# Ones multiplied in the early waits of TensorE, and a new order of 4,646 steps, in an attention and gated-MLP kernel

## The chip, the cores and the metric

The kernel runs as one program on one core of a Trainium2 chip. The metric is the device time of one execution in microseconds (us). A change is judged by the median of several executions.

## The reference

For each of 8 batches: attention over 8 heads of 576 tokens with 64 numbers each, in which only scores within tau of a row's maximum are kept, and then a gated MLP on the joined heads (576 x 512).

```python
scores = scale * np.matmul(q, k.transpose(0, 1, 3, 2))
thresh = np.max(scores, axis=-1, keepdims=True) - tau
scores = np.where(scores >= thresh, scores, -1000000000.0)
attn = softmax(scores)                    # over the last axis
x = np.matmul(attn, v)                    # heads joined: 576 x 512
h = gelu_tanh(x @ w_in)                   # 576 x 1024
u, v = h[..., :512], h[..., 512:]
v_n = layer_norm(v) * g_ln
gated = u * (np.einsum('ts,bsd->btd', w_sg, v_n) + b_sg[None, :, None])
out = x + gated @ w_out
```

## The kernel before, in words

The work of attention is cut into 32 pairs of heads, four pairs to a batch. A pair n goes through these steps, named as in the plan: q and k are loaded (L520) and v (L525); POOL scales q (q_scale, L528) and copies the last 64 tokens of both heads into one tile (L533); TensorE makes the scores in five blocks (s, L552, and the tail block, L559); VectorE (DVE) takes each block's row maxima (nm, L568), POOL turns them into thresholds (thr, L572), ScalarE (ACT) selects (sel, L582, which reads PSUM and frees the bank) and takes exponentials (exp, L588); DVE transposes 32 x 32 blocks (dt, L636); DMAs on SP's queue carry the transposed blocks to DRAM and back into other partitions (put, L646, and get, L653, in two parts: swa and swb); TensorE multiplies by v in two steps (pv, L667). The inverse sums take a way of their own: a small transpose (idt, L601), a write to DRAM (L606) and four reads back (L611, L618). DVE scales with them (rmul, L675 and L677), ACT and POOL split the result into a high and a low part (xh, L682; xl, L685; xt, L688). These x tiles of four pairs feed the batch's MLP, which TensorE works off in pieces of four products (L759), or for the first units of batch 0 in two parts (L775), so that the part on the first three pairs can go ahead of the fourth pair.

The weights w_in and w_out arrive as 64-bit words and are turned into pairs of 32-bit parts by ACT, POOL and DVE (L398 to L439); for six of the w_in tiles TensorE adds the parts with three products against identity matrices (w_sum, L430). All of this is done once, during the first 150 us.

Nothing schedules itself: the plan is a list of 4,646 steps, and the table ORDER gives the order in which their instructions are issued to the engines' queues; the table PLACES gives each TensorE step its PSUM bank or banks. Within an engine the instructions run in this order; across engines semaphores make them wait. Sixteen steps of the plan ("warm", L994) multiply a tile of ones with itself; nobody reads their result. They lie in columns 0 to 255 of a bank, which are also columns of the score blocks (columns 0 to 287), so that such a product waits for the reader of the scores that were there.

Of the kernel before, what the change touches and what calls it, by code (L numbers as in the profile page):

```python
# [12 lines left out]
F32 = mybir.dt.float32  # L13
# [7 lines left out]
P = 128  # L21
# [221 lines left out]
def tile_threshold_attention_gated_mlp(  # L243
# [15 lines left out]
    nc = tc.nc  # L259
# [15 lines left out]
    RG = P // BLK  # L275
    HB = BLK // 2
    MAINQ = NM * BLK
    PBUFS = 10
    COLS = 4
    GROUPS = 4  # L280
    PAIRS = CHUNKS // 2
# [711 lines left out]
    def warm_up(i):  # L993
        return lambda: nc.tensor.matmul(bank(f"warm{i}")[:, 0:256], warm[:, 0:P], warm, start=True, stop=True)  # L994
# [60 lines left out]
```

## Time and profile before

| | |
|---|---|
| median of 3 executions | 856.62 us (856.04 to 858.21) |
| the profiled execution | 859.3 us, span 857.5 us |
| TensorE (PE) busy | 815.6 us, 95% of the span |
| DVE, ACT, POOL busy | 632.2, 638.5, 467.2 us |
| mean granted TensorE clock | 0.992 |

The profiled execution is 2.7 us slower than the median. TensorE's busy time in 40 slices of 21.4 us is 7 or 8 tenths in five of the first six slices and 9 tenths or more in nearly all later ones. "PEld" is TensorE's loading of weights. Each product of 32-bit numbers shows as two records in the profile.

### The profile page before, as it was taken

What the parts mean: (1) busy time and instruction counts of PE and PEld (TensorE: products, weight loads), DVE (VectorE), ACT (ScalarE), POOL (GpSimd) and SP (SyncE); (2) the same over time, 40 slices, a digit from 0 to 9 for tenths busy, and PEclk for the clock granted to TensorE, in tenths of its full rate; (3) what the DMA queues carried; (4) which work ended last, traced back from release to release, by engine and by line L of the source; (5) the groups of instructions that cost most, each with busy time, mean ns of one, the idle gap of its engine ahead of it and who ended that gap; (6) DMA issues with size and microseconds to landing.
All of it is one profiled execution on the core that took longest, in us unless ns stands there. A gap on an engine that the chain in (4) does not pass through costs nothing.

```text
span 857.5 us, 24743 instructions
## 1 busy us (share of the span) xinstructions
PE 815.6 (95%) x9726; PEld 663.8 (77%) x9726; DVE 632.2 (74%) x1130; ACT 638.5 (74%) x1346; POOL 467.2 (54%) x797
## 2 busy tenths in 40 slices
PE   7787898999999899999999999999999989999998
PEld 4454677887888778887788878887688878888898
DVE  5998699776869477885878658884887738786255
ACT  6977588876979488895988768886798649877271
POOL 3786389443753465534664447534573347634283
PEclk9998999999999999999999999999999999999999
DMA  8898763885776934886558844888366953588401
GB/s 281 239 270 218 204 171 91 223 220 130 184 196 188 233 103 119 228 232 176 140 152 199 236 118 133 223 231 221 113 161 174 244 161 91 152 226 219 103 15 63
DMA packets 218998, 151.74 MB, mean 177 GB/s; under 512 B 32257, under 2 KB 204289, under 8 KB 218882
## 3 DMA queue, kind: packets, MB, share of 16 engines
q1 hardware_dynamic: 218882, 150.16, 65.5%
q8 instruction: 76, 1.25, 0.6%
q14 instruction: 40, 0.33, 0.1%
HBM read 97.68 MB, written 52.43 MB: 175 GB/s over the span
## 4 chain that ended last, share of the span: by engine, by line
PE 58%; DMA 14%; DVE 8%; POOL 6%; SPq 5%; issue 4%; ACT 4%; DVEq 0%; POOLq 0%; ACTq 0%
PE all_banks L759 34%; PE all_banks L552 11%; PE all_banks L667 9%; DMA pt<-swb 5%; DMA ir<-ird 3%; PE all_banks L559 3%; DVE columns L568 3%; DVE pt L636 2%; SPq L653 2%; DMA swb<-pt 2%; SPq L646 2%; DMA ird<-ir 1%; ACT p L582 1%; ACT p L588 1%; DMA out_T<-ot 1%
## 5 line engine op out<-in xcount | busy, mean ns | idle before, releaser
L568 DVE TENSOR_REDUCE columns<-all_banks 128x1 f32<-128x576 f32 x288 | 206.3, 745 | 70.2 <-PE all_banks L552 50.8
L582 ACT ACTIVATE p<-all_banks,columns 128x576 f32<-128x576 f32 x288 | 201.8, 737 | 70.9 <-POOL columns L572 69.5
L636 DVE STREAM_TRANSPOSE pt<-p 128x576 f32<-128x576 f32 x288 | 208.2, 753 | 22.0 <-ACT p L588 15.2
L588 ACT ACTIVATE p<-p,columns 128x576 f32<-128x576 f32 x288 | 220.9, 771 | 0.6
L552 PE MATMUL all_banks<-rk,rq 64*64 64x288 f32 x2048 | 165.9, 417 | 10.4 <-ACT p L582 6.0
L667 PE MATMUL all_banks<-pt,rv 64*64 64x128 f32 (+1 forms) x4608 | 158.1, 284 | 11.6 <-DMA pt<-swb 9.8
L667 PEld LDWEIGHTS all_banks<-pt,rv 64*64 64x64 f32 x4608 | 145.0, 133 | 25.5 <-issue 13.1
L572 POOL TENSOR_TENSOR columns<-columns 128x2 f32<-128x2 f32 (+1 forms) x160 | 35.0, 219 | 205.7 <-DVE columns L568 204.3
L552 PEld LDWEIGHTS all_banks<-rk,rq 64*64 64x64 f32 x2048 | 77.4, 133 | 63.3 <-ACT p L582 20.2
L759 PE MATMUL all_banks<-wsh,z 128*128 128x288 f32 (+2 forms) x512 | 114.2, 303 | 2.1 <-DVE uu L738 1.5
L759 PE MATMUL all_banks<-x,wi 128*128 128x288 f32 (+2 forms) x720 | 115.1, 300 | 0.0
L759 PE MATMUL all_banks<-wi,x 128*128 128x512 f32 (+1 forms) x424 | 112.9, 402 | 0.9 <-POOL x L685 0.8
L759 PEld LDWEIGHTS all_banks<-x,wi 128*128 128x128 f32 x720 | 101.1, 188 | 13.5 <-issue 5.9
L759 PE MATMUL all_banks<-gh,wo 128*128 128x288 f32 (+1 forms) x480 | 107.3, 301 | 2.3 <-DVE ir L677 2.0
L967 POOL TENSOR_TENSOR ot<-ot,x 128x288 f32<-128x288 f32 x112 | 89.6, 804 | 22.5 <-ACT ot L976 17.7
L759 PEld LDWEIGHTS all_banks<-wsh,z 128*128 128x128 f32 x512 | 83.9, 188 | 13.4 <-issue 6.1
L759 PEld LDWEIGHTS all_banks<-wi,x 128*128 128x128 f32 (+1 forms) x424 | 74.5, 185 | 22.9 <-issue 4.4
L759 PEld LDWEIGHTS all_banks<-gh,wo 128*128 128x128 f32 x480 | 79.4, 188 | 13.1 <-issue 5.7
L759 PE MATMUL all_banks<-wsl,z 128*128 128x288 f32 (+2 forms) x256 | 74.9, 299 | 0.0
L759 PE MATMUL all_banks<-gl,wo 128*128 128x288 f32 (+1 forms) x240 | 70.4, 298 | 0.0
L685 POOL TENSOR_TENSOR x<-ir,x 128x576 fp32r<-128x576 f32 x32 | 45.6, 1424 | 42.8 <-ACT x L682 41.4
L682 ACT ACTIVATE x<-ir 128x576 fp32r<-128x576 f32 x32 | 21.8, 682 | 50.3 <-DVE ir L677 45.6
(161 smaller groups left out, 1142.6 us busy)
## 6 DMA issues: line engine op xcount, KB each, us to landing
rv<-in_vP SPq DMA_DIRECT2D x32, 576.0 KB, 5.1
swb<-pt SPq DMA_DIRECT2D x32, 360.0 KB, 3.8
swb<-pt SPq DMA_DIRECT2D x64, 180.0 KB, 3.6
pt<-swb SPq DMA_DIRECT2D x64, 180.0 KB, 4.7
pt<-swb SPq DMA_DIRECT2D x32, 360.0 KB, 5.3
rq<-in_qT SPq DMA_DIRECT2D x32, 288.0 KB, 4.2
rk<-in_kT SPq DMA_DIRECT2D x32, 288.0 KB, 4.6
swa<-pt SPq DMA_DIRECT2D x32, 288.0 KB, 4.3
```

Source lines behind the costliest of these rows:

```text
L552: nc.tensor.matmul(st["s", h, i][cols, a, 0:HALF], st["q"][rows, i * P + c * D:i * P + (c + 1) * D], st["k"][rows, a * HALF:(a + 1) * HALF ...
L559: nc.tensor.matmul(sc[:, a, 0:HALF], tails[part], st["k"][:, a * HALF:(a + 1) * HALF], start=True, stop=True)
L568: return lambda: nc.vector.tensor_reduce(nm, st["s", h, i][:, :, 0:HALF], AX.XY, ALU.max, negate=True)
L572: return lambda: nc.gpsimd.tensor_tensor(nt, nm, toff[:, 0:1] if i == NM else toff, ALU.subtract)
L582: nc.scalar.activation(halves(st["p", h, i]), st["s", h, i][:, :, 0:HALF], AF.Prelu, bias=columns_of(i)[1][:, h:h + 1], alpha=BIG)
L588: return lambda: nc.scalar.activation(st["p", h, i], st["p", h, i], AF.Exp, bias=toff[:, 0:1], accum_out=l_of[part][:, c:c + 1])
L636: nc.vector.transpose(out, st["p", h, i].rearrange("p (j x) -> p j x", x=BLK))
L667: nc.tensor.matmul(st["acc"][h * D:(h + 1) * D, r, :, c0:c0 + w], v[rows, c, h], x[:, :, h * w:(h + 1) * w], start=(c == 0), stop=(c == PA ...
L682: nc.scalar.activation(xh_of[b, hp], st["ir"], AF.Copy)
L685: nc.gpsimd.tensor_tensor(xl_of[b, hp], st["ir"], xh_of[b, hp], ALU.subtract)
L759: nc.tensor.matmul(st["acc"][0:rows[0]] if rows else st["acc"], w, x, start=(j == 0), stop=(j == n - 1))
L967: return lambda: nc.gpsimd.tensor_tensor(o(), o(), x[b, m][:, ts_], ALU.add)
```

## The change

ORDER is replaced as a whole by another order of the same 4,630 other steps, and PLACES by other banks. The plan now has 120 steps of ones, of which the new ORDER issues 57 in place of 16. Each is half as wide (128 columns), has a tile of its own, and writes the last 128 columns of a bank, which no score block uses.

```diff
-    160 16 18 162 17 6 19 161 3 0 10 1 8 14 9 7 166 167 168 61 176 62 178 164 64 169 177 173 170 179 163 63 11 192 180
...
-    0101010102046002446023246045440264204634026406206240642602462024606245026546723530652605467052062046520672074205
...
+    7777777777777777777777770246777702336401126406204670276437724607777777247706240620642460777777777724260462104216
...
+    WARM = 120
...
-    warm = mtmp.tile([P, FH], F32, tag="mt1", name="warm")[:, 0:256]
+    warm = cpool.tile([P, P], F32, name="warm")
     nc.vector.memset(warm, 1.0)
 
     def warm_up(i):
-        return lambda: nc.tensor.matmul(bank(f"warm{i}")[:, 0:256], warm[:, 0:P], warm, start=True, stop=True)
-
-    for i in range(16):
+        return lambda: nc.tensor.matmul(all_banks[:, bank_of(1), 512 - P:512], warm, warm, start=True, stop=True)
+
+    for i in range(WARM):
         at("warm", i, warm_up(i))
```

Every engine's order differs a little everywhere: of TensorE's 976 other steps 142 keep their place, and a step moves by 4.6 places in the mean. The three places that matter for what follows:

TensorE at the start of the program, before (rk and rq are k and scaled q of pairs 0 and 1):

```order
L994 MATMUL all_banks<-warm 128x256 x9
L552 MATMUL all_banks<-rk_129,rq_125 64x288 x16
L994 MATMUL all_banks<-warm 128x256
L552 MATMUL all_banks<-rk_129,rq_125 64x288 x8
L994 MATMUL all_banks<-warm 128x256
L552 MATMUL all_banks<-rk_129,rq_125 64x288 x8
L559 MATMUL all_banks<-rk_129,tails_110 128x288 x2
```

and now, with ACT's first selections behind it and what they wait for:

```order
L997 MATMUL all_banks<-warm 128x128 x24
L555 MATMUL all_banks<-rk_148,rq_145 64x288 x16
L997 MATMUL all_banks<-warm 128x128 x4
L555 MATMUL all_banks<-rk_148,rq_145 64x288 x8
L997 MATMUL all_banks<-warm 128x128 x2
L555 MATMUL all_banks<-rk_148,rq_145 64x288 x8
```

```order
L585 ACTIVATE p_0_0_194<-all_banks,columns 128x576 [waits Pool_49]
L585 ACTIVATE p_1_0_201<-all_banks,columns 128x576 [waits DVE_49]
L591 ACTIVATE p_0_0_194,l_117<-p_0_0_194,columns 128x576 [waits Activation_49]
L591 ACTIVATE p_1_0_201,l_117<-p_1_0_201,columns 128x576 [waits Activation_49]
L585 ACTIVATE p_1_1_228<-all_banks,columns 128x576 [waits PE_49,Pool_49]
```

Nine wide products ahead of the first scores became 24 narrow ones. The four behind the second block of scores wait on DVE for a maximum of the scores in the same bank, and the last row's selection from that bank waits on TensorE for one of them.

TensorE around the values of pair 2 (pt_2, rv_849 and rv_851; L430, now L433, is w_sum), before:

```order
L430 MATMUL all_banks<-wi_815,minus 128x512
L552 MATMUL all_banks<-rk_795,rq_654 64x288 x8
L667 MATMUL all_banks<-pt_2_581,rv_849 64x2x64 x36
L667 MATMUL all_banks<-pt_2_768,rv_849 64x2x80 x36
L552 MATMUL all_banks<-rk_795,rq_654 64x288 x8
L430 MATMUL all_banks<-wz_569,ident_r 128x512 x2
L430 MATMUL all_banks<-wi_962,minus 128x512
L559 MATMUL all_banks<-rk_795,tails_110 128x288 x2
```

and now:

```order
L555 MATMUL all_banks<-rk_802,rq_795 64x288 x8
L997 MATMUL all_banks<-warm 128x128 x10
L433 MATMUL all_banks<-wz_468,ident_r 128x512 x2
L433 MATMUL all_banks<-wi_905,minus 128x512
L670 MATMUL all_banks<-pt_2_606,rv_851 64x2x64 x36
L555 MATMUL all_banks<-rk_802,rq_795 64x288 x8
L670 MATMUL all_banks<-pt_2_779,rv_851 64x2x80 x36
L433 MATMUL all_banks<-wz_382,ident_r 128x512 x2
L433 MATMUL all_banks<-wi_947,minus 128x512
L555 MATMUL all_banks<-rk_802,rq_795 64x288 x8
L562 MATMUL all_banks<-rk_802,tails_110 128x288 x2
```

Ten products of ones and a w_sum now stand ahead of the first value step; a block of scores moved between the two value steps; the w_sum and one block of scores stand behind them, with the tail block last.

SP's queue from the write of pair 3's inverse sums on, before:

```order
L606 DMA ird_1078<-ir_1076 128x32
L653 DMA pt_3_1003<-swb_1023 64x9x160
L653 DMA pt_3_1003<-swb_1023 32x9x160 x2
L611 DMA ir_1076<-ird_1078 64x4x128
L520 DMA rq_1161<-in_qT 128x576
L611 DMA ir_1076<-ird_1078 64x4x128
L618 DMA ir_1076<-ird_1078 64x4x16 x2
```

and now:

```order
L609 DMA ird_1100<-ir_1093 128x32
L656 DMA pt_3_1001<-swb_1048 64x9x160
L656 DMA pt_3_1001<-swb_1048 32x9x160 x2
L621 DMA ir_1093<-ird_1100 64x4x16
L614 DMA ir_1093<-ird_1100 64x4x128 x2
L621 DMA ir_1093<-ird_1100 64x4x16
```

The load of a later q, which stood between the reads of the inverse sums, moved behind them.

## Rows read from the trace of the kernel before

**Rows 1.** The page: busy time of each engine.
```profile
PE 815.6 (95%) x9726; PEld 663.8 (77%) x9726; DVE 632.2 (74%) x1130; ACT 638.5 (74%) x1346; POOL 467.2 (54%) x797
```
**Rows 2.** Busy time by stretch: stretch, its length, each engine, TensorE's clock, DMA, GB/s.
```profile
0.00:150.00 150.00, 126.90 (x1394) 85.17 (x1395) 125.86 (x214) 112.80 (x228) 99.08 (x162) 0.95 0.77 210
150.00:850.00 700.00, 684.91 (x8307) 575.09 (x8306) 502.17 (x908) 525.73 (x1119) 368.08 (x636) 1.00 0.64 170
850.00:857.50 7.50, 3.77 (x29) 3.51 (x27) 4.19 (x10) 0.00 (x0) 0.00 (x0) 1.00 0.35 122
```
**Rows 3.** The same view, the three stretches at half the clock.
```profile
49.20:52.60 3.40, 3.40 (x18) 1.68 (x18) 3.04 (x6) 2.08 (x5) 3.40 (x6) 0.50 0.93 299
69.70:76.50 6.80, 5.05 (x21) 2.48 (x22) 4.98 (x10) 5.81 (x12) 6.08 (x10) 0.50 0.90 246
107.20:110.60 3.40, 3.40 (x8) 2.72 (x9) 2.38 (x4) 2.07 (x5) 3.32 (x5) 0.51 0.60 104
```
**Rows 4.** TensorE's waits from 150 us on: us in total, times, longest.
```profile
PE all_banks L667 <- DMA pt<-swb: 8.6, 12, 1.6
```
**Rows 5.** Line L994 by stretch (PE, PEld, clock, DMA, GB/s), and its weight loads (ns).
```profile
1.20:4.80 3.60, 3.60 (x9) 2.89 (x10) 1.00 0.64 123
4.80:7.10 2.30, 2.30 (x11) 1.73 (x9) 1.00 1.04 349
...
L994 PEld LDWEIGHTS all_banks<-warm x32: 186/190/338, 1.2 to 23.4; 128*128 128x128 f32 x32
```
**Rows 6.** TensorE in order of time: start, us, instructions, idle time before and releaser.
```profile
48.67 2.82 PE L552 MATMUL all_banks<-rk,rq 64*64 64x288 f32 x16 [1.18 <-ACT p L582]
...
71.45 2.29 PE L559 MATMUL all_banks<-rk,tails 128*128 128x288 f32 x4 [2.39 <-ACT p L582]
73.67 2.20 PE L552 MATMUL all_banks<-rk,rq 64*64 64x288 f32 x16
...
84.66 1.18 PE L552 MATMUL all_banks<-rk,rq 64*64 64x288 f32 x16
...
87.83 1.13 PE L559 MATMUL all_banks<-rk,tails 128*128 128x288 f32 x4
```
**Rows 7.** DVE in order of time, its waits for TensorE between 50 and 80 us.
```profile
53.34 0.76 DVE L568 TENSOR_REDUCE columns<-all_banks 128x1 f32<-128x576 f32 x1 [0.30 <-PE all_banks L559]
...
73.85 0.76 DVE L568 TENSOR_REDUCE columns<-all_banks 128x1 f32<-128x576 f32 x1 [0.44 <-PE all_banks L559]
75.99 1.42 DVE L568 TENSOR_REDUCE columns<-all_banks 128x1 f32<-128x576 f32 x2 [1.38 <-PE all_banks L552]
...
79.83 1.42 DVE L568 TENSOR_REDUCE columns<-all_banks 128x1 f32<-128x576 f32 x2 [0.51 <-PE all_banks L552]
```
**Rows 8.** The chain that ended last, 68 to 112 us: start, us, what.
```profile
68.94 1.35 POOL x L685
...
84.87 0.97 PE all_banks L552 x16
85.84 2.15 PE all_banks L430 x5
87.99 0.98 PE all_banks L559 x4
...
89.74 0.68 DVE wt13h L408
...
90.57 6.28 DMA ird<-ir
...
97.58 0.97 SPq L520
...
99.91 4.71 DMA ir<-ird
...
107.20 2.07 PE all_banks L775 x4
...
110.89 1.18 PE all_banks L775 x9
```

More of the change, by code (lines that the diff above doesn't have):

```diff
@@ L31 @@
 ORDER = [int(i) for i in """
[194 rows of a table removed]
[196 rows of a table added]
 """.split()]
 PLACES = "".join("""
-    0101010102046002446023246045440264204634026406206240642602462024606245026546723530652605467052062046520672074205
-    6402562062016420264602345640262067205402602754025042062360530654320620642560230652064520602675204052026046720564
-    0256720340642016245621062506202645062306542062605423062606201465264106250162340246072401264162450626020467240762
-    0470264072340604672034602540623670450246202650126420564206205206742602464023674064040246204572042601642364064560
-    2304670423074062401640216420641264516206720562340625012673403460246046301642146234604623046306242605672301212374
-    65301624705215342070
+    7777777777777777777777770246777702336401126406204670276437724607777777247706240620642460777777777724260462104216
+    0230462302640763112470432046230467204304724072046402640236402467016426426456201462526106251262467452610261526426
+    0462104267024620472045620702040652360645260350164620260142064231642064204672064702402047236024604206465026740126
+    5142670460245620142612467427024206470276402704624017246426721042624176457026526042642106423062460426026405625062
+    4065235066306604672043402640142672420456205472046023402642016240260456252064724023406203043724501762074206240246
+    7024701246204207420674062406723012741456270531645207247563276
 """.split())
```

389 rows, old and new, of the table ORDER are left out of this document.

## The prediction

> **What bounds the kernel now.** I read the page first: TensorE is busy 95% of the span, the next engine 74% [rows 1], so TensorE's own work sets the time, and a change can only win what TensorE loses: idle time, time at half the clock, and products of ones. The table of stretches says where that is [rows 2]. In the first 150 us TensorE stands idle for 150 - 126.9 = 23.1 us; in the 700 us after that for 700 - 684.9 = 15.1 us; in the last 7.5 us for 3.7 us, which is the end of the last outputs. Early, DVE is nearly as busy as TensorE (125.9 us of 150): the four pairs of batch 0 must go through attention before any full MLP piece can run, and the weights are made beside them.
>
> In three early stretches the granted clock is 0.50, that is 1.2 in place of 2.4 GHz: 49.2 to 52.6, 69.7 to 76.5 and 107.2 to 110.6 us [rows 3]. Each follows a wait of TensorE, for instance 2.39 us idle before 71.45 [rows 6]. What it costs shows in the lengths: a tail block takes 2.29 us there and 1.13 us at full clock, a block of scores 2.20 against 1.18 us [rows 6]. Later, TensorE's largest wait is for the reads of swb before the second value step: 8.6 us in 12 waits [rows 4].
>
> **The change, part by part.** The sum of the other work is the same on every engine, so the terms are waits and clock.
>
> *The start.* A record of a 256-column product takes 3.6/9 = 0.40 us until 4.8 us and 2.3/11 = 0.21 us after that [rows 5]: the engine begins slowly and the rate doubles at 4.8 us, though the row's clock column shows 1.00 for both. Half the columns should take half: 0.20 and 0.105 us. The 24 products are 48 records: 18 in the first 3.6 us, the other 30 in 3.1 us, an end at 7.9 us where the old nine end at 7.1. The first scores follow directly: +0.8 us. Lower bound 0, if q or k lands as late as that. Upper bound: if the weight load (186 ns at its shortest [rows 5]) sets the pace, 30 x 0.186 = 5.6 us and +3.3 us. I take +0.8: a wide record already ran in 0.21 us, close to its load, so nothing shows that loads limit it further.
>
> The Trainium skill, "TensorE: Matmul & The Clock Gate", Part 1 on the clock gate, says that the number of slow products at a kernel's start varies from run to run of the same kernel (6, 11 or 14 in one). By it the +0.8 would be no fixed number; this trace shows one start only.
>
> *The clock in the middle.* The other 33 products stand in front of scores and w_sums between the first scores and about 120 us, most of them (9 and 10) near the waits that precede the first two slow stretches. If they keep the clock up, TensorE gets back half of its busy time there, (3.40 + 5.05)/2 = 4.2 us [rows 3]. Not all of it lies on the path, since DVE is then the engine that sets the pace. What DVE waited for TensorE in and behind these stretches is 0.30 + 0.44 + 1.38 + 0.51 = 2.6 us [rows 7], and I take that, bounds 0 and 4.2. One cause of the second stretch goes as well: POOL made the low part of pair 1's x (1.35 us [rows 8]) ahead of a threshold that ACT waited for; in the new order it stands behind the thresholds. This is the same wait, so it isn't counted twice. The third stretch (1.7 us) has no products near it; I leave it as it is: 0, bound -1.7.
>
> *What the filling costs.* At full rate 33 products are 66 x 0.105 = 6.9 us. They are hidden where TensorE would wait anyway. They don't run freely, though: the first of a group waits for DVE's maximum of the scores in its bank, and ACT's selection from that bank waits for a product of the group. I cost this at 0, covered by waits of 1.18 and 2.39 us [rows 6] and their like; uncovered it is the main rival.
>
> *Pair 3, which releases the MLP.* The path from the small transpose of pair 3 to the first pieces on its x is a DMA write (6.28 us with its landing), the reads (4.71 us) and the split, up to 107.20 [rows 8]. SP's load of a later q sat between these reads and took 0.97 us; it moved behind: -1.0 us, bounds 0 and -1.0. The small transpose waits in DVE's order for maxima of pair 4. Before, 0.97 + 2.15 + 0.98 us of TensorE stood between the second value step of pair 2 and these scores, and a maximum and a weight operation (0.68 us each) behind: 5.5 us. Now it is one w_sum and one block (2.15 + 1.2) and two maxima (1.4): 4.7 us, so -0.8, bound 0. On the other side, TensorE did one group more before that wait, nine products of a first MLP unit (1.18 us at full clock [rows 8]); now they come later: +1.2 us.
>
> *From 150 us on.* The reads that TensorE waits for, 8.6 us in 12 waits [rows 4], come after each pair's last transposes. I counted what TensorE has to do between these and the second value step, at the 0.13 us per product that nine in 1.18 us give [rows 8]. For the last pairs of seven batches, where no other work can be put in, it is 71 us before and 76 us now, 0.7 us more for each. All of it would be -4.9 us; but the cover is only one of several things that set these waits, so I take less than half, -2.0. Bounds: -8.6, all gone, and +3, a third of as much again, since every step moved.
>
> Sum: +0.8 - 2.6 - 1.0 - 0.8 + 1.2 - 2.0 = **-4.4 us**. The profiled execution took 859.3 us and would take 854.9; it is 2.7 us above the median, and against the median of 856.6 the forecast is **852.2 us**.
>
> **The rivals.** *The filling becomes a delay* (slower). A group of products that waits for DVE's maximum starts late, and everything behind it on TensorE waits too: the ten of the middle stand ahead of a w_sum and of pair 2's value steps, in the busiest stretch of DVE. Price: none of the 33 covered, +6.9 us, with the other terms of the first 150 us (-2.4) and nothing won later: 856.6 + 4.5 = 861.1. It decides where a wait is shorter than its products: seven take 1.5 us, the wait before the same block was 1.18 [rows 6]. For it speaks that the waits fall with the clock that is kept up; against it, that 23 us of idle time is three times the price.
>
> *No change.* TensorE's work stays, DVE's sum up to pair 3 stays within a microsecond, and the -2.0 of the late part turns out +0.4 or more: 854.1 to 859.2, about 856. For it speaks that all the early terms are small and of both signs. A variant: the start stays at the slow rate through all 24 products, 48 x 0.20 = 9.6 us and an end at 10.8, 3.7 us later; that makes the sum -1.5, 855.1. That a start has no fixed number of slow products is what the page of the Trainium skill cited above says.
>
> *More than forecast.* The reads are covered from 150 us on (-8.6) and the third slow stretch goes too (-1.7): 856.6 - 4.4 - 6.6 - 1.7 = 843.9. For it speaks that the same engine waits are at the same places in each batch; against it the small gain in cover.
>
> **How the numbers follow.** A measurement of this kernel can tell about 0.3%, 2.6 us, from no change. The forecast (847 to 854.0 us) has a chance of 0.47, more than forecast 0.11, no change with its variant 0.26, the filling as a delay 0.16. Faster is 0.58, the same 0.26, slower 0.16. The range leaves out the best of the large gains and most of the slower case: 846 to 859.5.
>
> **What would show it.** Right: no stretch at clock 0.50 before 105 us; DVE's waits for L568 between 50 and 80 us nearly gone; the first scores at about 7.9 us; the first piece on pair 3's x at 103 to 106 us; waits for swb after 150 us below 8 us in total. Wrong: groups of products of ones with idle time before them that DVE's maxima end; ACT waiting for L997; the first scores at 10 us or later; idle time of more than 17 us between 150 and 850 us.

## The result, and the profile after

The changed kernel takes 866.68 us (median of 16 executions, 862.02 to 869.98), the kernel before 860.38 us in as many executions on the same chip (856.04 to 865.8). The ratio is 1.0074, 95% interval 1.0051 to 1.0097: **slower by 0.7%, about 6.3 us**. The forecast was 4.4 us faster, and its range (846 to 859.5) does not hold the result. The 856.62 us that I started from came from three executions; the median of 16 is 3.8 us higher. That is a reason to set ratios above absolute times, but not the reason for the miss.

The profiled execution took 868.68 us, its span 866.9. Page, busy time of each engine [rows 1]:

```profile
PE 821.5 (95%) x9808; PEld 673.3 (78%) x9808; DVE 634.4 (73%) x1130; ACT 639.2 (74%) x1346; POOL 468.5 (54%) x797
```

Busy time by stretch (columns as in [rows 2]), the last two cut where the outputs end:

```profile
0.00:150.00 150.00, 124.36 (x1394) 89.23 (x1395) 115.14 (x196) 103.76 (x207) 90.97 (x149) 0.92 0.73 201
150.00:858.00 708.00, 691.79 (x8377) 578.97 (x8377) 513.88 (x921) 535.46 (x1141) 377.57 (x649) 1.00 0.65 170
858.00:866.90 8.90, 5.35 (x41) 5.14 (x39) 5.39 (x14) 0.00 (x0) 0.00 (x0) 0.94 0.33 114
```

The loss is in the first row. TensorE's busy time there is 2.5 us less than before, although 57 narrow products of ones run in it in place of 16 wide ones; DVE did 10.7 us less of its work, ACT 9.0 us less. Every engine is behind. From 150 us on TensorE idles for 16.2 us of 708, as before (15.1 of 700).

The same view, the stretches at half the clock [rows 3]:

```profile
22.78:26.19 3.41, 3.06 (x28) 1.28 (x20) 2.14 (x4) 3.02 (x8) 0.63 (x2) 0.50 1.00 220
33.02:39.84 6.82, 5.54 (x78) 4.72 (x76) 4.47 (x8) 5.38 (x11) 3.24 (x5) 0.50 1.01 269
53.50:60.32 6.82, 3.99 (x22) 3.53 (x26) 3.22 (x6) 3.53 (x7) 6.09 (x8) 0.50 0.63 184
84.22:91.04 6.82, 5.95 (x22) 5.10 (x23) 3.88 (x7) 1.43 (x5) 3.54 (x6) 0.50 0.78 196
```

23.9 us in place of 13.6, and sooner. What TensorE waited for in the first 125 us (in total, times, longest):

```profile
PE all_banks L997 <- DVE columns L571: 16.9, 6, 5.2
PE all_banks L555 <- ACT p L585: 3.4, 3, 2.1
```

And TensorE in order of time (start, us, instructions, idle time before and its releaser; two records to a product):

```profile
1.07 7.82 PE L997 MATMUL all_banks<-warm 128*128 128x128 f32 x48 [1.07 <-DVE warm L994]
8.82 2.17 PE L555 MATMUL all_banks<-rk,rq 64*64 64x288 f32 x32
...
56.33 3.36 PE L997 MATMUL all_banks<-warm 128*128 128x128 f32 x14 [5.12 <-DVE columns L571]
59.62 1.52 PE L555 MATMUL all_banks<-rk,rq 64*64 64x288 f32 x16
...
85.09 4.63 PE L997 MATMUL all_banks<-warm 128*128 128x128 f32 x20 [5.18 <-DVE columns L571]
89.51 2.65 PE L433 MATMUL all_banks<-wz,ident_r 128*128 128x512 f32 x4
...
118.15 1.19 PE L778 MATMUL all_banks<-wi,x 128*128 128x512 f32 x4 [0.76 <-POOL x L688]
```

The products of ones do not run while TensorE waits; they are what waits. The seven ahead of a block of pair 2's scores stand idle for 5.12 us until DVE has a maximum, and then take 3.36 us at half the clock. The ten ahead of a w_sum do the same for 5.18 and 4.63 us. The first piece on pair 3's x starts at 118.15 us, 11 us later than before [rows 8]. The delay goes on to the other engines. DVE waits for the scores behind the seven products, and ACT, whose next step in order copies the w_sum's result out, for the w_sum behind the ten:

```profile
61.28 1.42 DVE L571 TENSOR_REDUCE columns<-all_banks 128x1 f32<-128x576 f32 x2 [3.00 <-PE all_banks L555]
```

```profile
92.43 0.60 ACT L438 ACTIVATE wi<-all_banks 128x512 fp32r<-128x512 f32 x1 [6.78 <-PE all_banks L433]
```

### The profile page after: what moved, and what is told of

The parts are those of the page before. It is cut to its first block, busy times and chain, and to the rows that moved or that the text cites. A ratio compares the mean times of both kernels' runs of the same rounds, so it can differ in the third digit from the quotient of the medians.

```text
span 866.9 us, 24929 instructions
## 1 busy us (share of the span) xinstructions
PE 821.5 (95%) x9808; PEld 673.3 (78%) x9808; DVE 634.4 (73%) x1130; ACT 639.2 (74%) x1346; POOL 468.5 (54%) x797
## 4 chain that ended last, share of the span: by engine, by line
PE 56%; DMA 12%; DVE 9%; POOL 8%; ACT 6%; issue 4%; SPq 3%; POOLq 0%; DVEq 0%; ACTq 0%
PE all_banks L762 31%; PE all_banks L555 10%; PE all_banks L670 10%; DVE columns L571 3%; DMA pt<-swb 3%; DVE pt L639 3%; DMA swb<-pt 2%; PE all_banks L562 2%; DMA ir<-ird 2%; PE all_banks L997 2%; DMA out_T<-ot 2%; ACT p L591 2%; DMA ird<-ir 1%; POOL vv L870 1%; ACT p L585 1%
## 5 line engine op out<-in xcount | busy, mean ns | idle before, releaser
L555 PE MATMUL all_banks<-rk,rq 64*64 64x288 f32 x2048 | 163.3, 419 | 5.2 <-ACT p L585 4.0
L555 PEld LDWEIGHTS all_banks<-rk,rq 64*64 64x64 f32 x2048 | 75.0, 134 | 56.0 <-ACT p L585 16.2
L762 PE MATMUL all_banks<-wi,x 128*128 128x512 f32 x424 | 113.2, 400 | 3.0 <-POOL x L688 2.5
L762 PE MATMUL all_banks<-wsh,z 128*128 128x288 f32 (+2 forms) x512 | 114.0, 304 | 1.7 <-ACT z L876 0.7
L762 PE MATMUL all_banks<-gh,wo 128*128 128x288 f32 (+1 forms) x480 | 107.2, 301 | 4.3 <-ACT ot L979 2.4
L762 PEld LDWEIGHTS all_banks<-wi,x 128*128 128x128 f32 x424 | 73.3, 184 | 24.1 <-POOL x L688 5.2
L870 POOL TENSOR_TENSOR vv<-vv,g_bc 128x512 f32<-128x512 f32 (+1 forms) x40 | 52.4, 1311 | 8.0 <-ACT vv L867 7.3
```

The source lines that it names most:

```text
L555: nc.tensor.matmul(st["s", h, i][cols, a, 0:HALF], st["q"][rows, i * P + c * D:i * P + (c + 1) * D], st["k"][rows, a * HALF:(a + 1) * HALF ...
L762: nc.tensor.matmul(st["acc"][0:rows[0]] if rows else st["acc"], w, x, start=(j == 0), stop=(j == n - 1))
L870: nc.gpsimd.tensor_tensor(st["v", i], st["v", i], g_bc[0:rows], ALU.mult)
```

## The experiments

Theory 1: the products wait for DVE's maxima and hold up what stands behind them. Theory 2: the new order of the other steps is the slower one, and the products are innocent. Each run has 12 executions (e5 six), beside executions of the kernel before on the same chip. The medians of the kernel before lie between 858.96 and 860.38 us over the chips, so the ratios are surer than differences between medians. This table sums them up. Products: at the start + later. "Half clock" is the sum, in the first 150 us, of the stretches at half the clock, read in windows of 0.25 us, so that it differs a little from the sums above; "x" is the start of the first piece on pair 3's x; these two are of one profiled execution.

| run | products | median us | ratio to before (95%) | half clock | x |
|---|---|---|---|---|---|
| before | 9 + 7 wide | 860.38 | 1 | 13.5 | 107.2 |
| after | 24 + 33 | 866.68 | 1.0074 (1.0051 to 1.0097) | 23.8 | 118.2 |
| e1 | 24 + 0 | 860.47 | 1.0000 (0.9971 to 1.0028) | 13.8 | 107.9 |
| e2 | 24 + 16 | 864.45 | 1.0058 (1.0027 to 1.0088) | 24.3 | 111.3 |
| e7 | 24 + 10 | 868.14 | 1.0093 (1.0056 to 1.0130) | 27.0 | 112.8 |
| e10 | 24 + 33, other banks | 860.27 | 1.0009 (0.9976 to 1.0042) | 13.5 | 111.4 |
| e8 | 12 + 0 | 857.08 | 0.9970 (0.9935 to 1.0006) | 13.5 | 106.3 |
| e14 | the same | 857.39 | 0.9969 (0.9942 to 0.9996) | 27.3 | 108.3 |
| e11 | none | 856.19 | 0.9962 (0.9936 to 0.9988) | 13.8 | 105.1 |
| e17 | the same | 856.21 | 0.9973 (0.9946 to 1.0001) | 20.3 | 107.4 |
| e13 | 48 + 0 | 865.50 | 1.0072 (1.0045 to 1.0098) | 27.5 | 114.0 |
| e12 | 12 + 33, other banks | 858.67 | 0.9989 (0.9959 to 1.0019) | 20.5 | 111.3 |
| e5 | after, then before | 869.12 | 1.0120 (1.0075 to 1.0166) | 24.3 | 117.5 |
| e6 | before, then after | 860.92 | 1.0015 (0.9985 to 1.0044) | 17.3 | 107.5 |
| e9 | before, 9 + 0 | 860.77 | 1.0014 (0.9980 to 1.0049) | 17.0 | 107.7 |
| e15 | before, none | 862.15 | 1.0027 (1.0003 to 1.0051) | 26.5 | 109.3 |
| e16 | as e5, none | 857.46 | 0.9985 (0.9960 to 1.0009) | 24.0 | 107.2 |

**Run e1: no products behind the first scores.**

```diff
+DROP = range(24, 57)
...
             for i in ORDER:
-                plan[i].fn()
+                if i in DROP:
+                    next(places)
+                else:
+                    plan[i].fn()
```

> The changed kernel without its 33 products of ones behind the first scores; the 24 ahead of them and every other step and bank stay. Theory 1 (the products wait for DVE's maxima and hold up what stands behind them on TensorE): most of the loss comes back, 855 to 860 us, the first piece on pair 3's x at 107 to 110 us in place of 118. Theory 2 (the new order of the other steps in the first 150 us is the slower one, and the products only fill waits that are there anyway): 864 to 868, that piece at 115 or later, and the waits that DVE's maxima end appear as waits for ACT's selections of about the same length.

860.47 us, at the upper end of what theory 1 allowed (855 to 860), with the piece on pair 3's x where it put it: the whole loss against the kernel before comes back (1.0000), 6.2 us against the changed kernel, and theory 2 falls. The two places of above (this kernel's lines stand one or two higher):

```profile
52.09 2.82 PE L556 MATMUL all_banks<-rk,rq 64*64 64x288 f32 x16 [4.88 <-ACT p L586]
...
76.63 3.66 PE L434 MATMUL all_banks<-wz,ident_r 128*128 128x512 f32 x4 [2.92 <-ACT p L586]
...
107.89 1.98 PE L779 MATMUL all_banks<-wi,x 128*128 128x512 f32 x4 [0.77 <-POOL x L689]
```

TensorE waits there without products too, but for ACT, for 4.88 in place of 5.12 us ahead of pair 2's scores and for 2.92 in place of 5.18 us ahead of the w_sum.

**Run e2: only the small groups stay** (e1's edit, as in the following runs, with another list).

```diff
+DROP = (*range(36, 43), *range(45, 55))
```

> The changed kernel without the two largest groups, the seven products ahead of the scores of pair 2 and the ten ahead of a w_sum and pair 2's values: 40 of 57 products stay. Theory 1: these two groups waited 5.12 and 5.18 us and ran 3.36 and 4.63 us, so they carry most of the loss: 857 to 862 us. If the small groups matter as much: 863 to 865. Theory 2: 865 to 868.

864.45 us, the second case: by the medians the sixteen products in small groups carry 4.0 of the 6.2 us. They matter; whether more than the big groups, the intervals don't tell. Their own time is short (0.4 to 1.2 us a group); their waits aren't:

```profile
12.37 1.16 PE L998 MATMUL all_banks<-warm 128*128 128x128 f32 x8 [1.22 <-DVE columns L572]
...
16.26 0.71 PE L998 MATMUL all_banks<-warm 128*128 128x128 f32 x4 [1.60 <-DVE columns L572]
...
21.73 0.71 PE L998 MATMUL all_banks<-warm 128*128 128x128 f32 x4 [2.46 <-DVE columns L572]
```

So the wait and the products' own time had to be told apart, which the next two runs do from both sides.

**Run e7: one product of each of the ten groups.**

```diff
+DROP = (25, 26, 27, 29, 31, 35, *range(37, 43), 44, *range(46, 55), 56)
```

> The changed kernel with one product of ones left of each of the ten groups behind the first scores, 23 of the 33 taken away: every wait for a maximum and every wait of a selection for a product stays, the products' own time goes down to a third. Theory 1a (the waits for DVE's maxima cost, since they end later than the releases by ACT that the next step needs): 864 to 867 us, close to the changed kernel. Theory 1b (the products' own time costs: the wait that they were to fill has ended when they may start, and at half the clock they are slow): about a third of the 6.2 us between the kernel without them and the changed one is left, 861 to 863.

**Run e10: all products, 29 of the 33 later ones in banks of the step behind them.** The bank is now one that the next step needs anyway: 0 for products 24 to 27, 6 for 28 and 29, 2 for 30 and 31, 0 for 32, 6 for 33, 2 for 36 to 42, 0 for 43 and 44, 2 for 45 to 54. Products 34, 35, 55 and 56 keep their banks.

```diff
+MOVED = {24: 0, 25: 0, 26: 0, 27: 0, 28: 6, 29: 6, 30: 2, 31: 2, 32: 0, 33: 6, 36: 2, 37: 2,
...
-        return lambda: nc.tensor.matmul(all_banks[:, bank_of(1), 512 - P:512], warm, warm, start=True, stop=True)
+        return lambda: nc.tensor.matmul(all_banks[:, MOVED.get(i, bank_of(1)), 512 - P:512], warm, warm, start=True, stop=True)
```

> All 57 products of the changed kernel, but 29 of the 33 behind the first scores write a bank of the step that stands behind them, so that they wait for the same release by ACT as that step and no longer for a maximum of their own. Theory 1a: the loss goes, 860 to 862 us. Theory 1b: the products still run only when the next step could, 864 to 868 us.

Ten products that wait cost 7.7 us over e1 (868.14), 33 that don't wait on a maximum cost nothing that can be measured (860.27). The two ran on the same chip, and the intervals of their ratios lie apart. The same two places and TensorE's waits in the first 125 us, in e7

```profile
55.13 0.80 PE L998 MATMUL all_banks<-warm 128*128 128x128 f32 x2 [4.55 <-DVE columns L572]
...
82.01 0.80 PE L998 MATMUL all_banks<-warm 128*128 128x128 f32 x2 [5.18 <-DVE columns L572]
```

```profile
PE all_banks L998 <- DVE columns L572: 15.9, 6, 5.2
```

and in e10:

```profile
15.29 0.71 PE L998 MATMUL all_banks<-warm 128*128 128x128 f32 x4 [0.48 <-ACT p L586]
...
19.48 0.71 PE L998 MATMUL all_banks<-warm 128*128 128x128 f32 x4 [0.71 <-ACT p L586]
...
53.38 3.35 PE L998 MATMUL all_banks<-warm 128*128 128x128 f32 x14 [5.16 <-ACT p L586]
...
79.61 3.73 PE L998 MATMUL all_banks<-warm 128*128 128x128 f32 x20 [2.92 <-ACT p L586]
```

```profile
PE all_banks L998 <- ACT p L586: 11.3, 6, 5.2
```

What differs is whose release the product needs. PLACES puts most products into bank 7, and where they wait their bank holds scores of the newest block: the seven (products 36 to 42) and the ten (45 to 54) both wait for the maximum of a head that lies in banks 6 and 7, issued just ahead of them. The step behind them goes to bank 2, whose scores are a block older and which ACT frees sooner. A product in the newest block's bank ties TensorE to the end of DVE's queue, without one TensorE runs a block ahead. From after to e10 the wait ahead of the w_sum shrinks from 5.18 to 2.92 us and the second and third early ones from 1.60 and 2.46 to 0.48 and 0.71. The first early one grows from 1.22 to 1.61, and the one ahead of pair 2's scores stays, 5.12 and 5.16: there ACT's release comes hardly sooner than DVE's maximum. The products touch columns that no scores use and wait all the same, and in another bank they wait for another release: the dependence is kept by bank. The Trainium skill, "PSUM — Partial Sum Buffer", section "PSUM bank collisions raise a hardware error", gives the reason: two engines must not touch one bank (in the same 32 partitions) at a time, whatever the columns, so guards go by bank. No run here shows such a collision. e10 takes away two waits together, the product's for a maximum and the selection's for a product (2.7 us of ACT's waits in the first 150 us after); they weren't tried apart.

How the waits become time at the end isn't shown. Against e1 the piece on pair 3's x is 3.4 us late in e2, 4.9 in e7, 3.5 in e10 and 10.3 in after, the medians 4.0, 7.7, -0.2 and 6.2 us: e2 and e10 are equally late there and differ by 4.2 us at the end. From that piece to the end of the span the profiled executions take 752.8 us in e1, 755.3 in e7, 745.6 in e10 and 748.8 in after. So the products' own time delays that piece as well (e10), but it doesn't reach the total, and why not is open.

**Runs e8 and e14 (12 at the start, none later, twice), e11 and e17 (none at all, twice), e13 (48).** For e8 and e14, then e11 and e17, then e13 beside e1's edit:

```diff
+DROP = range(12, 57)
```

```diff
+DROP = range(57)
```

```diff
+ORDER = [*range(57, 81), *ORDER]
 PLACES = "".join("""
+    777777777777777777777777
```

> The changed kernel without the 33 later products and with 12 in place of 24 at the start. In the kernel with 24 the first scores start at 8.78 us, and scaled q is ready at about 5.7 us. If the start lies on the path: 12 products end at about 6 us, the first scores start at 5.9 to 6.5, and the time falls by 2 to 3 us to 857.5 to 858.5. If the later steps pace the first pairs anyway: 860 to 861. If the lower number keeps the slow rate on for longer: the first scores take over 3 us in place of 2.17, and 860 to 862.

> The kernel with 12 products at the start and none later once more (857.1 us in 12 runs, 0.3% below the kernel before, interval -0.65 to +0.06%). If that gain is real: 855.5 to 858.5. If it was chance: 859 to 861, as the kernel before.

> The changed kernel with no product of ones at all. With 24 at the start it took 860.5 us, with 12 it took 857.1. Scaled q is ready at 5.6 us. If only the time of the first scores counts: they start at 5.6 to 6.0 and the total is 855.5 to 857.5. If TensorE needs work before them to come out of its slow rate: the first block of scores takes 3.5 to 4.3 us in place of 2.2 to 2.5, the gain over 12 products is lost and the total is 857 to 861.

> The new order without products once more: 855 to 857.5 us if the 0.4% below the kernel before were no chance, 858 to 860 if they were.

> The changed kernel without the 33 later products and with 48 in place of 24 at the start, the suspected cost doubled. If the start lies on the path: 24 more products are 48 records of 0.105 to 0.15 us, the first scores start at 13.5 to 16 us, and the total is 864 to 868, 4 to 7 above the 860.5 with 24. If something else paces the first pairs: 860 to 862.

None, 12, 24 and 48 products at the start give 856.2, 857.2, 860.5 and 865.5 us: what stands ahead of the first scores beyond the first 12 products is paid for; between none and 12 no difference can be told. TensorE's first instructions in e8, e11, e12 (of which more below) and e13:

```profile
1.07 5.49 PE L998 MATMUL all_banks<-warm 128*128 128x128 f32 x24 [1.07 <-DVE warm L995]
6.49 2.46 PE L556 MATMUL all_banks<-rk,rq 64*64 64x288 f32 x32
```

```profile
6.24 3.93 PE L556 MATMUL all_banks<-rk,rq 64*64 64x288 f32 x32 [6.24 <-DMA rk<-in_kT]
...
105.06 1.20 PE L779 MATMUL all_banks<-wi,x 128*128 128x512 f32 x4 [0.77 <-POOL x L689]
```

```profile
6.92 2.17 PE L557 MATMUL all_banks<-rk,rq 64*64 64x288 f32 x32 [1.33 <-DMA rk<-in_kT]
```

```profile
1.07 13.44 PE L1000 MATMUL all_banks<-warm 128*128 128x128 f32 x96 [1.07 <-DVE warm L997]
14.44 1.93 PE L558 MATMUL all_banks<-rk,rq 64*64 64x288 f32 x28
```

Without products the first block is slow (3.93 us against 2.17 in after), so the condition that I named is met, but the total is not worse for it: the block still ends at 10.2 us, against 11.0 behind 24 products. Behind 12 it ends at 9.0 us, and that doesn't show in the total either (a difference of 1 us can't be told here). The traces say why the first 12 cost so little: without products TensorE waits for the load of k until 6.24 us (6.51 in e17), and 12 products end at 6.49 us or, in e12, ahead of that load. Those beyond 12 come after it. At the w_sum whose wait e1 has ended at 76.63 us, TensorE goes on at 74.60 and 75.60 us with 12 products (e8, e14), at 75.05 and 76.29 with none (e11, e17) and at 83.54 with 48: taking products away at the start brings 0.3 to 2.0 us there. The 3 to 4 us between the medians of e1 and these four runs are more than that, and where the rest lies is open. By the ratios e8, e14, e11 and e17 are all 0.3 to 0.4% below the kernel before; two of the four intervals exclude 1, the other two end just above it.

**Run e12: both, 12 at the start and 33 in the banks of the next step** (e10's edit and this).

```diff
+DROP = range(12, 24)
```

> 12 products at the start, and the 33 later ones in the banks of the steps behind them as in the run before with all 57 (860.3 us). If the two effects add: 856 to 858.5, as with 12 and none later. If the later products' own time counts now that the start is shorter: 859 to 861. If they win something by the clock they keep up: below 855.5.

858.67 us, just above the sum of the two and below the case of a price. Inconclusive: the interval holds 12 products alone as well as 2 us more. There is no sign of a gain by the clock.

**Runs e5 and e6: halves of the two orders.** ORDER and PLACES of one kernel up to step 1434 (e5) or 1385 (e6) of its order, at about 215 us, then the other's.

> The order and the banks of the changed kernel up to the second batch's second half (about 215 us), those of the kernel before from there on. Theory 1 and theory 2 both put the loss into the first 120 us: 867 to 870 us, 7 to 9 above the kernel before. Theory 3 (the early delay is absorbed, and the new late order is the slower one): 859 to 862.

> The other way round: the order, banks and 16 wide products of the kernel before up to about 215 us, the new order from there on. Theories 1 and 2: the late part won 1.5 us by the two profiles (pair 3's piece to the end 750.3 us before, 748.8 after): 858 to 860 us, 0 to 2 below the kernel before. Theory 3: 864 to 868.

869.12 and 860.92: the loss comes from the early part. The late part is worth 2.4 us between e5 and after, -0.6 between e6 and before.

**Runs e9, e15, e16: the old products taken away.** e9 and e15 in the kernel before (the seven later ones, and all), e16 in e5's order:

```diff
+DROP = (11, 15, 5, 4, 2, 12, 13)
```

```diff
+DROP = range(16)
```

```diff
+DROP = range(57)
```

> The kernel before without its seven later products of ones (the nine ahead of the first scores stay). They wait 3.4 us for ACT and run for 4 us there. Theory 1b holds for them too: 858 to 860 us, 0.5 to 2 below the kernel before. If they keep the clock up as they were meant to: a stretch at half the clock appears before 45 us, and 861 to 864.

> The kernel before without its 16 products of ones. If the gain of the new order without products (856.2 us, -0.4%) is the start alone: 856 to 858.5. If the new order of the other steps makes it: 859 to 861.

> No products of ones; the new order and banks up to about 215 us, the old ones from there on. If the late part of the new order is worth the 2.0 us that I gave it: 857.5 to 859.5, 1 to 3 above the new order without products. If it is worth nothing: within 1 us of that.

The old order is slower without any of its products: 862.15 us, by 0.27%, at the edge of what can be told. And a stretch at half the clock appears at 23.6 us, where [rows 3] has none before 49.2 (e15, busy time by stretch):

```profile
23.60:33.60 10.00, 9.01 (x38) 4.23 (x39) 8.22 (x16) 8.45 (x17) 6.41 (x13) 0.50 0.76 224
51.00:54.20 3.20, 3.11 (x6) 2.01 (x7) 2.48 (x5) 2.16 (x5) 1.74 (x4) 0.52 1.01 297
71.40:78.00 6.60, 6.42 (x23) 3.01 (x24) 4.78 (x9) 6.57 (x15) 4.80 (x9) 0.50 0.90 227
```

In e15 TensorE waits 3.30 us for POOL there, in the kernel before three wide products stand in that wait, and the tail block starts no later, at 24.02 against 24.34 us:

```profile
22.46 1.56 PE L994 MATMUL all_banks<-warm 128*128 128x256 f32 x6 [1.74 <-ACT p L582]
24.02 1.24 PE L559 MATMUL all_banks<-rk,tails 128*128 128x288 f32 x4
```

```profile
24.34 2.29 PE L560 MATMUL all_banks<-rk,tails 128*128 128x288 f32 x4 [3.30 <-POOL tails L534]
```

Filling is free at this place, where the product's release comes before that of the next step. That it wins time is not shown: with the seven later ones alone taken away (e9) the stretch at half the clock comes as well, from 24.3 to 34.5 us, but the time stays, 860.77. e6, with the early order and the products of the kernel before, has like that kernel no such stretch before 48 us; so two executions with these products and two without agree, and there are no more. e16 is 1.25 us above e17, the third look at the late part.

## Why the prediction was wrong

The medians, from several chips and each uncertain by 2 to 3 us, make a chain: the old order without products 862.2, with its 16 about 860.4 (-1.8); the new order without products 856.2 (-6.0 from the old one without; -0.54%, 4.6 us, by the ratios of e15 and e17, which ran on the same chip), with 24 at the start 860.5 (+4.3), with all 57 866.7 (+6.2). The rearrangement alone beat its own terms (-1.0 - 0.8 + 1.2 - 2.0 = -2.6 us); the products lost more than it won.

- **The failed step is "What the filling costs", 0.** It measures 6.2 us (e1). I had seen that the first of a group waits for DVE's maximum and that a selection waits for a product, and then took the waits of the kernel before [rows 6] as cover. But a wait covers a product only if the product may start when the wait begins. Here its release came later than that of the step behind it, so it made the wait longer, most of all ahead of the w_sum (5.18 us, 2.92 without products). Ahead of pair 2's scores both releases come at nearly the same time (5.12 and 4.88 us): there the products don't lengthen the wait, but start only at its end, and their 3.36 us come behind it. The question I left out was: which bank, whose reader, and when does that reader run against what the next step needs? The order of the steps and the banks in PLACES had the answer.
- **The rival that came true was priced by the wrong quantity.** "The filling becomes a delay" said 861.1, from 6.9 us of the products' own time. e7 has a third of that time and the whole loss, e10 all of it and no loss that the time shows; only the piece on pair 3's x comes 3.5 us later in e10 than in e1. That the rival's price and the loss of 6.2 us lie close together is chance.
- **The start, +0.8, was too small.** The first scores came at 8.82 us, not at 7.9, 1.75 later than before. I let the rate of records double at 4.8 us; in after it was still 6 in the 0.9 us up to 5.7. And I compared with the old nine only: the 12 that fit into the wait for k, or none, would have been better. The lower bound that I gave, k landing as late as the products' end, did not come: k was there at 6.24, 6.51 and 6.92 us in e11, e17 and e12. The doubling in e13 confirms the place: first scores 5.7 us later than in e1, total 5.0 us later.
- **The clock in the middle, -2.6, had the wrong sign**: 23.9 us at half the clock for 13.6, the first scores' successors stand in a slow stretch from 22.8 us on, and DVE's wait behind the seven products is 3.00 us in place of nearly gone. How much of the loss is the clock's is not shown: two executions of one kernel, e8 and e14, have 13.5 and 27.3 us of it and spans of 854.0 and 855.1 us. Among the kernels with 24 products at the start much half clock and a loss go together (after, e2 and e7 against e1 and e10), so the clock stays a rival for part of it; against it, e14 and e16 have as much half clock (27.3 and 24.0 us) and no loss.
- **Pair 3's path, -1.8 and +1.2, has the right sign where the products don't cover it**: I expected the first piece on its x at 103 to 106 us; it came at 105.06 and 107.40 in the new order without products, one of the two inside, and at 109.27 in the old order without them. The three terms were not tried one by one.
- **The late reads, -2.0, are the right way and smaller than the runs can settle.** TensorE's waits for swb after 150 us fell as expected, from 8.6 us in 12 waits [rows 4] to

```profile
PE all_banks L670 <- DMA pt<-swb: 3.1, 4, 1.2
PE all_banks L762 <- POOL x L688: 2.5, 3, 1.0
PE all_banks L762 <- ACT ot L979: 2.4, 1, 2.4
```

  but other waits took their place: the late part is worth 2.4, -0.6 and 1.25 us in the three looks, each uncertain by about 3.
- **Of the signs that I named**, those for a wrong forecast came: groups of products with idle time that maxima end, ACT behind a product. The other two did not come: the first scores stood at 8.82 us, not at 10, and TensorE's idle time after 150 us is 16.2 us, not more than 17. Without products the same order has no such wait, and about the time that I forecast for the change as a ratio: -0.27 and -0.38% against my -0.5%.

Where the remaining gain of the new order over the old one lies (4.6 to 6.0 us without products; 2 to 4 at pair 3's x in single executions, about 1 late) is open.

## What to carry to other kernels

Work that is to fill a wait must be ready sooner than the step behind it: look up what the filler itself waits for, and compare it with the release that the next instruction in the queue needs. On an in-order engine a filler with the later release doesn't fill the wait, it sets it; its length matters less than its dependence (ten that waited cost more here than 33 that didn't wait for DVE). If a buffer must be given to a filler, give it that of the next step, not that of the newest one, which here made it harmless, not useful (e10 against e1); and test fillers one group at a time and with none at all.

## What the runs showed of the hardware that I had not expected

- Products ahead of the first real work did not pay, and beyond those that ran while its data loaded they cost: the engine begins slowly (19 records of 128 columns in the 3.7 us up to 4.8 us, 22 in 2.3 us after 6.5), but a first block at the slow rate at 6.24 us ended before one at the full rate at 8.82.

```profile
1.07:3.07 2.00, 2.00 (x9) 2.00 (x10) 1.00 0.54 149
3.07:4.80 1.73, 1.73 (x10) 1.73 (x9) 1.00 0.84 167
4.80:5.70 0.90, 0.90 (x6) 0.90 (x5) 1.00 0.90 278
5.70:6.50 0.80, 0.80 (x10) 0.80 (x8) 1.00 0.98 382
6.50:8.80 2.30, 2.30 (x22) 2.20 (x20) 1.00 1.06 407
```

  (Line L997 of after by stretch: PE, PEld, clock, DMA share, GB/s.)
- The same 24 products end the start at different times: the first scores came at 8.82, 8.78, 8.98, 8.38, 7.97 and 8.74 us in after, e1, e2, e5, e7 and e10. The Trainium skill, "TensorE: Matmul & The Clock Gate", Part 1 on the clock gate, says that the number of slow products at a start varies from run to run; these traces agree: in after the full rate is reached at 5.7 us, in e7 already 9 records stand in the 0.73 us from 4.07 to 4.80 us.
- Stretches at half the clock vary between executions of one kernel (13.5 and 27.3 us, e8 and e14) without a like difference of the span: in this pair 13.8 us more of them came with 1.1 us more.
